# Attention beside a gated feed-forward layer: a shorter lead of row maxima, a lead job opened by the second lane, and new token orders

## The chip, the cores and the metric

The kernel runs on one core of a Trainium2 chip. A core has TensorE (PE in the profile; its weight loads are PEld), VectorE (DVE), ScalarE (ACT), GpSimd (POOL) and SyncE (SP), which here only issues DMAs. The metric is the device time of one execution in microseconds; lower is better.

## The reference

```python
# x: (1, 2048, 512), 32 heads of 16 that share one K and one V
q = (x @ wq) in heads;  k = x @ wk;  v = x @ wv
p = softmax(q k^T * 16 ** -0.5)          # per head, 2048 x 2048
a = (p v, heads side by side) @ wo
b = ((x @ w_gate) * (x @ w_up)) @ w_down # 1792 wide, no other nonlinearity
g = sigmoid((x * gate_w).sum(-1))
out = g * a + (1 - g) * b
```

## The kernel before

**Units.** The 2048 query rows are four chunks `c` of 512, each of four tiles `t` of 128. The 32 heads are four groups `g` of 8. A unit is (c, g, t), 64 in all. A unit's scores are computed twice. The first pass (`p1`, L800) multiplies queries by keys and lets DVE take the maximum of each row (L801, tile `mx`). The second pass (`p2`, L859) computes the transposed scores with the maximum subtracted: the negated maximum, in a high and a low part, stands as two more rows of `Q` beside the query, and the exponential is taken by ACT (L860, tile `P`). The product with V is `pv` (L872, tile `acc`).

**From the maxima to the second pass.** When 32 maxima of a unit are there (16 steps on each of two lanes), `p1_end` combines them on DVE (L809 to L815), four small DMAs store them to `dm` (L821), and two more fetch them into the extra rows of `Q` (L828). All of them go through SP's queue, which issues in order and waits at the first DMA that isn't ready. In the same queue stand the loads of weights (`wn`, `wdn`, L190), of queries (`Q<-dq`, L240), the stores of queries (`dq`, L224), the stores of the transposed x (`xd`, L373) and its reloads at a change of chunk (`xh`, `xl`, L213), and the steps of the softmax's division (`do`, `dn`, `raw`, `dr`, `rb`, L667 to L698).

**Lanes.** First and second pass need few contraction rows, so TensorE is used as two lanes: lane 0 takes rows 0 to 63, lane 1 rows 64 to 127, and the two run side by side. All other products (queries, gate, up, down, wo) are jobs of 12 steps a lane (L998, tile `ms`): each lane multiplies its half of the contraction rows, both add into one PSUM bank. Lane 0 opens a job's bank (`start`), lane 1 follows one job later and closes it (`stop`), then `evac` copies the bank out. So `count[1]` starts 12 steps after `count[0]`. The product with V takes all rows, so no lane runs beside it.

**The order of the work** is written out. One cycle of the token string `ORDER` covers one unit: `a`/`b` is a step of the first pass on lane 0/1, `c`/`d` one of the second pass, `e`/`f` a step of a job, `p` one round of `pv`. `APART` is a second string for cycles that take the jobs whose lanes write banks of their own. Runs of the first pass are ahead of the second: before the first cycle a lead loop puts `LEAD` steps of the first pass on each lane, six of them done earlier in the start-up, and beside them six jobs (`LEADJOBS`). In that loop a lane takes a step of the first pass whenever the planned DVE is less than 1.3 us behind, else a step of a job. In cycle u the second pass works on unit u and the first pass on what follows: with a lead of 25, the 16 steps of unit u + 1 are complete with the seventh `a` and `b` of the cycle. When the first pass runs out near the end, its tokens become job steps; after `npv` reaches `LASTORDER`, `end_token` chooses instead of the string.

**The planner.** While the program is written, a class `State` keeps planned times of lanes, DVE, ACT, POOL and banks, and a list of events puts DMAs and POOL work into the program order: `later(ns, fn)` and `at(t, fn)` issue `fn` once planned time has come. They set places in the queues, not waits on the chip. A second-pass token waits in planned time for `mat[u]`, the planned landing of the maxima, and a job is taken only if its weights are planned to be split (`ready`).

**Gate and up weights.** `order` lists (chunk, block of 128 columns). Job n has part 0 (gate) and part 1 (up). `ffn_stage` loads both weights, `ffn_split` splits each into a high and a low part on POOL (L152 and L153), and `evac` copies a part's result, multiplies the two on POOL (L599) and splits the product.

The tiles of `P` have 11 buffers (`PBUF`), those of `Q` five (`QB`).

Of the kernel before, what the change touches and what calls it, by code (L numbers as in the profile page):

```python
# [29 lines left out]
NJ = 16  # L30
# [1 line left out]
FG = 4  # L32
LAST = (0, 0, 1, 0, 1, 0)
YADDS = len(FGS) + 1 + sum(len(fs) < FG for fs in FGS)
LEAD = 25
PBUF = 11
WB = 4
QB = 5
# [17 lines left out]
SWAP = (10, 11, 12, 15)  # L56
LAT, LAT_LAST = 1.0, 0.5
LATE = 16
LEADJOBS = 6
O0, O1 = 0, 0  # L60


ORDER = (
    "cdebefedafebcfefcfcbefebedebcfefadefefcfafedebedebefedefadefcfafcfafefaf"
    "cfcdefebafedcpppbcbcbappdafafcfcfafafcfefedebedebefedebedefefafebadapppb"
)

APART = (
    "cedadfeeffaadfeedbedeedaffedeebedfcfacffafeefafcbfefccfafebcffceffabcfef"
    "ebefeedebbebapppbcdcdcppcbedfaeffcfadefefaebedeffcfadeebcfbeefbafedapppb"  # L70
)
SLOT = 1
COLS = (slice(0, 256), slice(256, 512))
# [6 lines left out]
def mix_kernel(ctx: ExitStack, tc: tile.TileContext, x, wq, wk, wv, wo, wg, wu, wd, gw, out):  # L80
    nc = tc.nc
# [111 lines left out]
    def w_split(n, tags, bufs, after=0.0):  # L193
        hi, lo = w512(tags[0], F32R, bufs), w512(tags[1], F32R, bufs)
        at = split2(hi, lo, n, after)
        return (hi, lo), at
# [20 lines left out]
    def at(t, fn):  # L217
        later(max(0.0, t - clock["T"]), fn)
# [9 lines left out]
    qat = {}  # L228
# [337 lines left out]
    def ffn_stage(i):  # L566
        if i < len(order):
            fs = slice(order[i][1] * 128, order[i][1] * 128 + 128)
            staged[i] = [stage(wg_v[:, :, fs]), stage(wu_v[:, :, fs])], clock["T"] + 4000.0

    def ffn_split(i):
        if i < len(order):
            ns, landed = staged.pop(i)
            W[i] = [w_split(n, ("wh", "wl"), WB, landed) for n in ns]
            at(W[i][1][1] + 300.0, lambda: ffn_stage(i + 2))

    def wd_split(wdn):
        if len(wdn) < 2:
# [2 lines left out]
    def ffn_job(n, i, gu, hat, wdn):  # L581
        c, f = order[n]

        def evac(p, part):
            gu[i] = w512("gs", F32, 3)
            if st["idle"]:
                nc.vector.tensor_copy(gu[i], p)
                end = spend("dve", RED)
            else:
                nc.scalar.copy(gu[i], p)  # L590
                end = spend("act", COPY)
            if len(gu) == 2:
                hf = w512("hf", F32, 1)
                h[f] = w512("hh", F32R, FG + 2), w512("hl", F32R, FG + 2)
                if st["idle"]:
                    nc.vector.tensor_tensor(hf, gu[0], gu[1], op=OP.mult)
                    spend("dve", 620.0, end + 200.0)
                else:
                    nc.gpsimd.tensor_tensor(hf, gu[0], gu[1], op=OP.mult)  # L599
                    spend("pool", 1240.0, end + 200.0)  # L600
                done = split2(h[f][0], h[f][1], hf)
                wd_split(wdn)
                wds[f], split_at = wdn[1]
                hat[f] = max(done, split_at) + 300.0
                if f == NF - 1 and c + 1 < NC:
                    x_turn(c + 1)
                ffn_split(n + 2)
                if n == len(order) - 4:
                    picks()
                    later(25000.0, wo_last)  # L610
        return Job(lambda: proj(W[n][i][0], xT[c]), evac,
                   lambda: max(W[n][i][1] + 300.0 if n in W else 1e18, xat.get(c, 1e18)))

    def down_jobs(c, fs, hat):
        n = FG // len(fs)
# [190 lines left out]
    def p1_end(u):  # L806
        q = Q[u]
        m = mm[u % 2]
        nc.vector.tensor_reduce(m[:, 0:8], mx.pop(u), axis=AX.X, op=OP.max)  # L809
        w = work.tile([128, 3, 32], F32R, name="mt", bufs=2)  # L810
        mt = w[:, 0].bitcast(F32)
        nc.vector.transpose(mt, m)
        nc.vector.tensor_reduce(w[:, 1], mt.rearrange("p (q v) -> p q v", v=1), axis=AX.X, op=OP.max, negate=True)
        with nc.allow_low_precision(reason="the low part of two that are kept"):
            nc.vector.tensor_reduce(w[:, 2], w[:, 0:2].bitcast(F32).rearrange("p v q -> p q v"), axis=AX.X, op=OP.add)  # L815
        end = spend("dve", 700.0)
        d = dram.tile([2, 8, 128], F32, name="dm", tag="dm", bufs=2)

        def store():
            for b in range(4):  # L820
                nc.sync.dma_start(d[:, :, b * 32:b * 32 + 32].rearrange("v c q -> c v q"),  # L821
                                  w[b * 32:b * 32 + 8, 1:3].bitcast(F32))
            later(3200, fetch)

        def fetch():
            for half in range(2):
                r = half * 64 + 48
                nc.sync.dma_start(q[r:r + 2].bitcast(F32), d[:, half * 4:half * 4 + 4, :])  # L828
            mat[u] = clock["T"] + 4000.0
        later(end - clock["T"] + 300.0, store)  # L830

    P = {}
# [124 lines left out]

    own, apart = {}, False

    def fill(l):  # L960

        c = count[l] + (O0, O1)[l]
        count[l] += 1
        k, i = c // 12 - l, c % 12
        wait = 0.0
        if i == 0 and l == 0:
            st["apart"] = apart and k % 3 == SLOT
            for _ in range(40):
                if peek():
                    break  # L970
                wait_ns(100.0)
            if peek():
                j = jobs[k] = take()
                j.items = j.prods()
                j.len = len(j.items) // j.parts
                if st["idle"]:
                    j.split()
                j.end, j.bank, j.p = [[None, None] for _ in range(j.parts)], {}, {}
            st["apart"] = False
        j = jobs.get(k)  # L980
        if j is None or i >= len(j.items):
            return
        part, i = divmod(i, j.len)
        if i == 0 and (l == 0 or j.apart):
            b = E.claim()
            wait, E.free[b] = E.free[b], 1e18
            j.bank[part] = b
            j.p[part] = ms_bank(b)
            if j.apart:
                own[l] = b, j.p[part]  # L990
        elif i == 0 and j.end[part][0] > E.known:
            fence()
        b, p = own[l] if j.apart else (j.bank[part], j.p[part])
        at = E.issue(l, wait)
        E.wrote[b] = E.seq
        lhs, rhs = j.items[part * j.len + i]
        end = i + 1 == j.len
        nc.tensor.matmul(p, lhs[HALVES[l]], rhs[HALVES[l]], start=(i == 0 and (l == 0 or j.apart)),  # L998
                         stop=(end and (l == 1 or j.apart)))
        if end:  # L1000
            j.end[part][l] = E.seq
            if part + 1 == j.parts and None not in j.end[part]:
                del jobs[k]
            if l == 1 or j.apart:
                clock["T"] = max(clock["T"], at)
                clock["act"], clock["dve"] = max(E.act, at + SEEN), max(E.dve, at + SEEN)
                if st["idle"]:
                    E.free[b] = clock["dve"] + RED_END + GAP
                    clock["act"] = E.act
                else:  # L1010
                    E.free[b] = clock["act"] + COPY_END + GAP
                    clock["dve"] = E.dve
                j.evac(p, part)
                E.act, E.dve = max(E.act, clock["act"]), max(E.dve, clock["dve"])
# [44 lines left out]
    def fillable(l):  # L1059
        c = count[l] + (O0, O1)[l]  # L1060
        if E.npv == 0 and count[l] >= 0 and min(E.n1) < LEAD:
            return False
        while st["idle"] and c % 12 and (c // 12 - l not in jobs or c % 12 >= len(jobs[c // 12 - l].items)):
            count[l] += 1
            c += 1
        if c % 12 == 0 and l == 0:
            return len(jobs) < (2 if min(E.n1) >= LEAD else 3) and peek() is not None
        j = jobs.get(c // 12 - l)
        if j is None or l == 0 or c % 12 % j.len > 0:
            return j is not None  # L1070
        end = j.end[c % 12 // j.len][0] if c % 12 < len(j.items) and not j.apart else 0
        return end is not None and end <= E.known

    count = [-12 * LEADJOBS - O0, -12 * (LEADJOBS - 1) - O1]
    while min(E.n1) < LEAD or min(count) < 0:
        l = 0 if E.nl[0] <= E.nl[1] else 1
        k = E.n1[l]
        some = k < LEAD and k <= E.n1[1 - l] + 2 and qat.get(order1[k][0], 1e18) <= clock["T"]
        if some and (E.dve < E.nl[l] + 1300.0 or not fillable(l)) and min(E.free) < E.nl[l]:
            token("ab"[l])  # L1080
        elif fillable(l):
            token("ef"[l])
        else:
            E.nl[l] += 30.0
            events_until(min(E.nl))
# [111 lines left out]
```

## Time and profile before

| what | us |
|---|---|
| median of 3 runs (lowest, highest) | 1596.78 (1596.07, 1596.89) |
| the profiled execution: its time, its span | 1597.58, 1595.6 |
| PE busy | 1590.0 |
| DVE busy, of this the row maxima (L801) | 1339.5, 1260.7 |
| ACT busy, of this the exponentials (L860) | 1203.5, 1067.8 |
| POOL busy | 719.5 |

The page names each group of instructions by line, engine, operation and tiles, with its count, busy time, the mean in ns, and what ended the engine's idle time before it. The granted TensorE clock is 0.999 of full speed. In the order of time a row has the start and the length in microseconds, and how many instructions are merged in it. A row of a stretch has the stretch, its length, the busy time of PE, PEld, DVE, ACT and POOL, each with its number of instructions, then the granted clock, the share of DMA time and GB/s. Matmuls overlap and their ends are modelled, so PE busy says little on how full its lanes are.

### The profile page before, as it was taken

How to read it: one execution, taken by the hardware profiler on the slowest of the kernel's cores; microseconds unless marked ns; L12 is line 12 of the kernel's file. 1: busy time of each engine (PE TensorE's matmuls, PEld its weight loads, DVE VectorE, ACT ScalarE, POOL GpSimd, SP SyncE). 2: the span in 40 equal slices, each digit the busy share in tenths (PEclk: the TensorE clock that was granted, in tenths of full speed). 3: DMA queues.
4: the chain of work that ended last, by engine and by line, in shares of the span. 5: the costliest groups of instructions: out<-in, count | busy, mean ns of one | idle time of the engine just before them, and what ended most of it. 6: DMA issues, size and time to landing. Idle time of an engine off the chain costs nothing.

```text
span 1595.6 us, 35607 instructions
## 1 busy us (share of the span) xinstructions
PE 1590.0 (100%) x13155; PEld 1046.0 (66%) x13155; DVE 1339.5 (84%) x2423; ACT 1203.5 (75%) x2360; POOL 719.5 (45%) x858
## 2 busy tenths in 40 slices
PE   9999999999999999999999999999999999999998
PEld 7766667666666666666666666666666666666664
DVE  6988888888888888888888888888888888888873
ACT  4577777777788777777788777777788777777775
POOL 3334653535643552534543650643743561553530
PEclk9999999999999999999999999999999999999999
DMA  4563322212311221212232221212231221221201
GB/s 157 188 205 112 107 62 65 57 54 78 116 54 51 76 75 45 76 49 61 80 101 62 77 69 50 77 49 63 77 102 48 74 73 55 66 67 42 56 29 46
DMA packets 185557, 121.68 MB, mean 76 GB/s; under 512 B 46378, under 2 KB 154998, under 8 KB 185384
## 3 DMA queue, kind: packets, MB, share of 16 engines
q1 hardware_dynamic: 184176, 119.21, 25.0%
q8 instruction: 104, 1.70, 0.5%
q14 instruction: 69, 0.57, 0.1%
q10 hardware_dynamic: 1208, 0.20, 0.1%
HBM read 82.96 MB, written 36.17 MB: 75 GB/s over the span
## 4 chain that ended last, share of the span: by engine, by line
PE 100%; DVE 0%; DVEq 0%; issue 0%
PE ms L998 36%; PE acc L872 29%; PE s L800 17%; PE s L859 16%; PE ms L165 1%; PE px L300 0%; PE px L285 0%; PE wo L1173 0%; PE warm L885 0%; PE pv L343 0%; PE warm L888 0%; DVE y L782 0%; DVEq L1193 0%; PE sums L752 0%; PE pv L355 0%
## 5 line engine op out<-in xcount | busy, mean ns | idle before, releaser
L801 DVE TENSOR_REDUCE mx<-s 128x1 f32<-128x512 f32 x2048 | 1260.7, 683 | 205.0 <-PE s L859 141.8
L860 ACT ACTIVATE P<-s 128x512 f32<-128x512 f32 x2048 | 1067.8, 630 | 196.2 <-PE s L800 95.8
L859 PE MATMUL s<-Q,KK 50*128 50x512 f32 x2044 | 713.7, 405 | 0.0
L800 PE MATMUL s<-KK,Q 48*128 48x512 f32 x2048 | 711.8, 406 | 0.2 <-issue 0.2
L872 PE MATMUL acc<-P,V 128*32 128x512 f32 x4096 | 480.1, 597 | 0.0
L800 PEld LDWEIGHTS s<-KK,Q 48*128 48x128 f32 x2048 | 347.4, 185 | 141.2 <-issue 46.8
L859 PEld LDWEIGHTS s<-Q,KK 50*128 50x128 f32 x2044 | 354.8, 185 | 85.7 <-issue 53.8
L998 PE MATMUL ms<-xh,wh 64*128 64x512 f32 x920 | 322.2, 394 | 0.0
L998 PE MATMUL ms<-xh,wl 64*128 64x512 f32 x920 | 321.9, 391 | 0.0
L998 PE MATMUL ms<-xl,wh 64*128 64x512 f32 x920 | 307.8, 391 | 0.0
L872 PEld LDWEIGHTS acc<-P,V 128*32 128x32 f32 x4096 | 113.4, 109 | 253.1 <-issue 232.7
L599 POOL TENSOR_TENSOR hf<-gs 128x512 f32<-128x512 f32 x56 | 72.0, 1285 | 372.3 <-ACT gs L590 361.2
L412 POOL TENSOR_TENSOR y<-y,yt 128x512 f32<-128x512 f32 x67 | 85.6, 1283 | 217.0 <-ACT yt L410 213.8
L998 PEld LDWEIGHTS ms<-xh,wh 64*128 64x128 f32 x920 | 161.4, 186 | 14.0 <-POOL wl L153 0.2
L998 PEld LDWEIGHTS ms<-xh,wl 64*128 64x128 f32 x920 | 159.4, 186 | 10.0
L998 PE MATMUL ms<-wdh,hh 64*128 64x512 f32 x448 | 159.7, 396 | 0.0
L998 PEld LDWEIGHTS ms<-xl,wh 64*128 64x128 f32 x920 | 154.0, 185 | 8.8
L998 PE MATMUL ms<-wdh,hl 64*128 64x512 f32 x448 | 158.0, 392 | 0.0
L998 PE MATMUL ms<-wdl,hh 64*128 64x512 f32 x448 | 155.3, 392 | 0.0
L153 POOL TENSOR_TENSOR wl<-wn,wh 128x512 fp32r<-128x512 f32 x117 | 150.7, 1288 | 9.4
L876 ACT COPY osb<-acc 128x512 f32<-128x512 f32 x64 | 37.6, 588 | 139.5 <-PE acc L872 139.5
L998 PEld LDWEIGHTS ms<-wdh,hh 64*128 64x128 f32 x448 | 79.7, 185 | 6.7 <-ACT P L860 0.4
(171 smaller groups left out, 1267.7 us busy)
## 6 DMA issues: line engine op xcount, KB each, us to landing
do<-osb SPq DMA_DIRECT2D x63, 256.0 KB
wn<-in_B_w_gate_dram SPq DMA_DIRECT2D x56, 256.0 KB
wn<-in_B_w_up_dram SPq DMA_DIRECT2D x56, 256.0 KB
wdn<-in_B_w_down_dram SPq DMA_DIRECT2D x56, 256.0 KB
Q<-dq SPq DMA_DIRECT2D x384, 32.0 KB
raw<-do SPq DMA_DIRECT2D x252, 32.0 KB
dq<-oh SPq DMA_DIRECT2D x16, 256.0 KB
dq<-ol SPq DMA_DIRECT2D x16, 256.0 KB
```

Source lines behind the costliest of these rows:

```text
L153: nc.gpsimd.tensor_tensor(lo, src, hi.bitcast(F32), op=OP.subtract)
L165: nc.tensor.matmul(p, l, r, start=start and i == 0, stop=stop and i == len(prods) - 1)
L412: nc.gpsimd.tensor_tensor(y[c, t], y[c, t], tmp, op=OP.add)
L599: nc.gpsimd.tensor_tensor(hf, gu[0], gu[1], op=OP.mult)
L800: nc.tensor.matmul(p, q[r, slot], KK[r, kq * 512:(kq + 1) * 512], start=True, stop=True)
L801: nc.vector.tensor_reduce(mx[u][:, half * 4 + slot, kq:kq + 1], p, axis=AX.X, op=OP.max)
L859: nc.tensor.matmul(p, kj, q[r].rearrange("p s q -> p (s q)"), start=True, stop=True)
L860: nc.scalar.activation(P[s][:, half], p, AF.Exp, scale=0.25)
L872: nc.tensor.matmul(acc[u][b:b + 32, :], V[:, j + i], src[:, half], start=(j == 0), stop=(j == NJ - 2))
L876: nc.scalar.copy(osb, acc.pop(u))
L998: nc.tensor.matmul(p, lhs[HALVES[l]], rhs[HALVES[l]], start=(i == 0 and (l == 0 or j.apart)), stop=(end and (l == 1 or j.apart)))
```

## The change

- `LEAD` is 21. The first 16 of these steps are taken as before; the other five are spread over the last 36 job steps of lane 0 (`PACED`), unless no job step can be issued.
- The lead jobs have an order per lane (`LEADS`). Lane 0 takes -6, -4, -3, -2, -5, -1, lane 1 takes -5, -6, -4, -3, -2 and, after the lead, -1. Job -5 is opened by lane 1 and closed by lane 0, which `first` tells in `fill` and `fillable`; all others are opened by lane 0 as before.
- Both strings are new. With a lead of 21, the steps of unit u + 1 are complete with the eleventh `a` and `b` of cycle u.
- The gate weights of job n + 2 are split on POOL at the first `evac` of job n, and the up weights at the second, ahead of the down weights.
- The planned time from storing the maxima to fetching them is 2600 and not 3200, and from there to their landing 3000 and not 4000.

```diff
-LEAD = 25
+LEAD = 21
+PACED = 36
-LEADJOBS = 6
+LEADS = (-6, -4, -3, -2, -5, -1), (-5, -6, -4, -3, -2, -1)
+LEADJOBS = len(LEADS[0])
 ORDER = (
-    "cdebefedafebcfefcfcbefebedebcfefadefefcfafedebedebefedefadefcfafcfafefaf"
-    "cfcdefebafedcpppbcbcbappdafafcfcfafafcfefedebedebefedebedefefafebadapppb"
+    "adadefebcfefadefcfebededafefcfebebcfefedafefedebedafefcbefededebcfebefcf"
+    "ebcfafafafcfafcfppcbfebcdefeebedefcbefcfebedefadefafafcfefadpppcdababppp"
 APART = (
-    "cedadfeeffaadfeedbedeedaffedeebedfcfacffafeefafcbfefccfafebcffceffabcfef"
-    "ebefeedebbebapppbcdcdcppcbedfaeffcfadefefaebedeffcfadeebcfbeefbafedapppb"
+    "dafcbedefeafedebdebeedebdefefcbefccfafaffcfafefdeafeffcebcfefbcfeafaffcf"
+    "eadefefcfafedfafeabfebapppcbadcbcppcbdebedeebedefefadefebcfedfedafecbppp"
...
-    def ffn_split(i):
+    def ffn_split(i, parts=range(2)):
         if i < len(order):
-            ns, landed = staged.pop(i)
-            W[i] = [w_split(n, ("wh", "wl"), WB, landed) for n in ns]
-            at(W[i][1][1] + 300.0, lambda: ffn_stage(i + 2))
+            ns, landed = staged[i]
+            for part in parts:
+                W.setdefault(i, []).append(w_split(ns[part], ("wh", "wl"), WB, landed))
+            if len(W[i]) == 2:
+                at(W[i][1][1] + 300.0, lambda: ffn_stage(i + 2))
...
+            if len(gu) == 1:
+                ffn_split(n + 2, (0,))
             if len(gu) == 2:
...
                 done = split2(h[f][0], h[f][1], hf)
+                ffn_split(n + 2, (1,))
                 wd_split(wdn)
...
-                ffn_split(n + 2)
...
-            later(3200, fetch)
+            later(2600, fetch)
...
-            mat[u] = clock["T"] + 4000.0
+            mat[u] = clock["T"] + 3000.0
...
+    def place(l):
+        c = count[l] + (O0, O1)[l]
+        k = c // 12 - l
+        if k < 0:
+            k = LEADS[l][k]
+        return k, c % 12, int(k == LEADS[1][0])
...
-        if i == 0 and (l == 0 or j.apart):
+        if i == 0 and (l == first or j.apart):
...
-            return len(jobs) < (2 if min(E.n1) >= LEAD else 3) and peek() is not None
+        k, i, first = place(l)
+        if i == 0 and l == first:
+            return (k < 0 or len(jobs) < 2) and peek() is not None
...
-        some = k < LEAD and k <= E.n1[1 - l] + 2 and qat.get(order1[k][0], 1e18) <= clock["T"]
+        due = NJ + (LEAD - NJ) * (1 + count[0] / PACED)
+        some = k < LEAD and (k < max(NJ, due) or not any(map(fillable, range(2)))) and k <= E.n1[1 - l] + 2 and qat.get(order1[k][0], 1e18) <= clock["T"]
```

More of the change, by code (lines that the diff above doesn't have):

```diff
@@ L611, in ffn_job @@
         return Job(lambda: proj(W[n][i][0], xT[c]), evac,
-                   lambda: max(W[n][i][1] + 300.0 if n in W else 1e18, xat.get(c, 1e18)))
+                   lambda: max(W[n][i][1] + 300.0 if len(W.get(n, ())) > i else 1e18, xat.get(c, 1e18)))
     def down_jobs(c, fs, hat):
@@ L958, in mix_kernel @@
     own, apart = {}, False
+    def place(l):
[4 more added lines that the diff above has]
+        return k, c % 12, int(k == LEADS[1][0])
     def fill(l):
-        c = count[l] + (O0, O1)[l]
+        k, i, first = place(l)
         count[l] += 1
-        k, i = c // 12 - l, c % 12
         wait = 0.0
-        if i == 0 and l == 0:
+        if i == 0 and l == first:
             st["apart"] = apart and k % 3 == SLOT
@@ L990, in fill @@
                 own[l] = b, j.p[part]
-        elif i == 0 and j.end[part][0] > E.known:
+        elif i == 0 and j.end[part][first] > E.known:
             fence()
@@ L997, in fill @@
         end = i + 1 == j.len
-        nc.tensor.matmul(p, lhs[HALVES[l]], rhs[HALVES[l]], start=(i == 0 and (l == 0 or j.apart)),
-                         stop=(end and (l == 1 or j.apart)))
+        nc.tensor.matmul(p, lhs[HALVES[l]], rhs[HALVES[l]], start=(i == 0 and (l == first or j.apart)),
+                         stop=(end and (l != first or j.apart)))
         if end:
@@ L1003, in fill @@
                 del jobs[k]
-            if l == 1 or j.apart:
+            if l != first or j.apart:
                 clock["T"] = max(clock["T"], at)
@@ L1065, in fillable @@
             c += 1
-        if c % 12 == 0 and l == 0:
-            return len(jobs) < (2 if min(E.n1) >= LEAD else 3) and peek() is not None
-        j = jobs.get(c // 12 - l)
-        if j is None or l == 0 or c % 12 % j.len > 0:
+        k, i, first = place(l)
+        if i == 0 and l == first:
+            return (k < 0 or len(jobs) < 2) and peek() is not None
+        j = jobs.get(k)
+        if j is None or l == first or i % j.len > 0:
             return j is not None
-        end = j.end[c % 12 // j.len][0] if c % 12 < len(j.items) and not j.apart else 0
+        end = j.end[i // j.len][first] if c % 12 < len(j.items) and not j.apart else 0
         return end is not None and end <= E.known
```

## The prediction

> **What bounds the kernel now.** I read the page first (shares of busy time, the chain that ended last, the costliest groups), then stretches of the span side by side, then the order of time around the lead, a cycle's end and a late maximum.
>
> ```profile
> PE 1590.0 (100%) x13155; PEld 1046.0 (66%) x13155; DVE 1339.5 (84%) x2423; ACT 1203.5 (75%) x2360; POOL 719.5 (45%) x858
> PE 100%; DVE 0%; DVEq 0%; issue 0%
> L801 DVE TENSOR_REDUCE mx<-s 128x1 f32<-128x512 f32 x2048 | 1260.7, 683 | 205.0 <-PE s L859 141.8
> L998 PEld LDWEIGHTS ms<-xh,wh 64*128 64x128 f32 x920 | 161.4, 186 | 14.0 <-POOL wl L153 0.2
> ```
>
> The chain that ended last lies on TensorE alone, so time is won only where its two lanes (row halves 0-63 and 64-127) are filled better. What a filled pair of lane steps costs, and what a whole cycle costs, is read here: first two neighbouring rows of the order of time with both lanes full, then stretches.
>
> ```profile
> 1580.73 0.45 PE L998 MATMUL ms<-wdh,hl 64*128 64x512 f32 x2
> 1580.96 0.45 PE L998 MATMUL ms<-wdl,hh 64*128 64x512 f32 x2
> ...
> 54.80:79.85 25.05, 25.05 (x203) 15.80 (x202) 21.84 (x38) 18.40 (x36) 7.69 (x9) 1.00 0.68 244
> ...
> 558.78:582.58 23.80, 23.80 (x206) 15.57 (x202) 20.48 (x37) 18.38 (x36) 19.22 (x22) 1.00 0.30 86
> 247.06:270.95 23.89, 23.89 (x204) 15.84 (x200) 20.52 (x37) 18.30 (x36) 9.26 (x11) 1.00 0.21 61
> 438.07:462.62 24.55, 24.55 (x204) 15.65 (x201) 20.63 (x37) 20.21 (x39) 10.88 (x12) 1.00 0.21 60
> ```
>
> A pair of steps takes 1580.96 - 1580.73 = 0.23 us. An ordinary cycle (one token string, one unit) takes 23.89, a good one 23.80, one with the APART string 24.55, and the first cycle 25.05. In all of them PE reads as 100% busy: the loss hides inside "busy", and only the length tells it.
>
> The lead, the stretch before the first cycle, is next: PE in two equal windows, PE's first and last steps of it, its transposes for V, then DVE.
>
> ```profile
> 32.10:38.10 6.00, 6.00 (x41) 4.99 (x41) 5.76 (x10) 1.16 (x4) 2.34 (x2) 1.00 0.00 0
> 38.10:44.10 6.00, 6.00 (x58) 5.79 (x56) 6.00 (x11) 0.94 (x4) 1.44 (x2) 1.00 0.02 5
> ...
> 32.09 0.49 PE L998 MATMUL ms<-xh,wh 64*128 64x512 f32 x1
> ...
> 37.69 0.27 PE L355 MATMUL pv<-ident,gs 64*128 64x64 f32 x1
> ...
> 38.18 0.47 PE L800 MATMUL s<-KK,Q 48*128 48x512 f32 x1
> ...
> 54.78 0.49 PE L859 MATMUL s<-Q,KK 50*128 50x512 f32 x1
> ...
> 32.66 12.16 DVE L801 TENSOR_REDUCE mx<-s 128x1 f32<-128x512 f32 x20 [0.23 <-PE s L800]
> ...
> 45.67 19.88 DVE L801 TENSOR_REDUCE mx<-s 128x1 f32<-128x512 f32 x32
> ```
>
> In the first 6 us PE issues 41 matmuls, in the next 6 us 58: lane 1 has no job yet, since it follows lane 0 by one job. DVE reduces without a break, 12.16 / 20 = 0.61 us a maximum. The lead runs from 32.09 to the first second-pass matmul at 54.78, 22.7 us.
>
> **The change, part by part.** The sum is made against the profiled execution, 1597.58 us (span 1595.6), which is 0.8 above the median of the three runs, 1596.78.
>
> *Lead of 21 and lane 1's own job.* Six steps of each lane are done before the lead, so it holds 21 - 6 = 15 maxima per lane and not 19, plus 72 job steps on lane 0 and 60 on lane 1. Lane 0 then needs 15 + 72 = 87 steps x 0.23 = 20.0, and 0.5 for the transposes (37.69 to 38.18): 20.5 us. DVE needs 30 x 0.61 = 18.3, so it isn't the limit any more (before: 38 x 0.61 = 23.2, about the 22.7 seen). The lead is 2.2 us shorter. The 4 maxima per lane left out of it are done later, where they push 4 pairs of job steps to the end: 4 x 0.23 = +0.9. Net **-1.3**. Ends: 0, if lane 1, with 12 fewer steps, idles as much at the end as it did at the start and lane 0 waits for DVE; -2.2, if the four steps fall into idle slots of the last cycles.
>
> *The first cycle* took 25.05 where a later one takes 23.89, so 1.2 too much, with DVE still working off the lead (the row of 32 reductions runs unbroken from 45.67 to 65.55). With DVE no longer the limit of the lead I take half, **-0.6**; ends 0 and -1.2.
>
> *New strings.* Both old and new ORDER have 144 tokens: 16 each of a, b, c, d, 36 of e, 36 of f, and 8 of p in three bursts. Nothing is added or removed, so the sum of work is the same and only stalls can change. They are bounded by the ordinary cycle against the good one: 23.89 - 23.80 = 0.09 a cycle, x 55 ordinary cycles (64, less the first, two at the end and six with APART) = -5.0. Upward the nearest row is an APART cycle: 24.55 - 23.89 = 0.66, x 55 = +36. What queues where can be counted off the strings. Before the first burst, the last 14 tokens (7 pairs, 1.6 us) held five exponentials and two maxima; now three and four. ScalarE's pile there is smaller, DVE's is larger, but the burst of matmuls that follows lets both drain. In the next stretch the first ten tokens held three maxima, after four in the six tokens of `bcbcba`; now two, right after a burst. The pile that a lane meets in mid-stretch is a bit lower, so I lean to the good cycle's row and take half of its gain, 0.045 x 55 = **-2.5**. The new APART has its six cycles' 0.66 to win or to double: 6 x 0.66 = 4.0 both ways, taken as 0.
>
> *The later maxima.* This is where the edit can hurt. Rows: an ordinary unit, a unit with the reload of x ahead of it in the queue, and an early unit. Each begins with the unit's last maximum (L800) and ends with the first second-pass matmul of that unit (L859).
>
> ```profile
> 231.42 0.39 PE L800 MATMUL s<-KK,Q 48*128 48x512 f32 x1
> ...
> 232.86 0.19 DVE L809 TENSOR_REDUCE mm<-mx 128x8 f32<-128x32 f32 x1
> ...
> 233.79 1.29 SPq L821 DMA_DIRECT2D dm<-mt  x4
> 236.12 0.53 SPq L828 DMA_DIRECT2D Q<-dm  x2
> ...
> 247.06 0.50 PE L859 MATMUL s<-Q,KK 50*128 50x512 f32 x1
> ...
> 1165.41 0.39 PE L800 MATMUL s<-KK,Q 48*128 48x512 f32 x1
> ...
> 1166.73 1.75 SPq L213 DMA_DIRECT2D xh<-xd  x4
> 1168.58 1.80 SPq L213 DMA_DIRECT2D xl<-xd  x4
> 1170.42 4.15 SPq L240 DMA_DIRECT2D Q<-dq  x6
> 1175.42 3.17 SPq L821 DMA_DIRECT2D dm<-mt  x4
> 1179.64 0.53 SPq L828 DMA_DIRECT2D Q<-dm  x2
> ...
> 1180.97 0.50 PE L800 MATMUL s<-KK,Q 48*128 48x512 f32 x1
> 1181.03 0.50 PE L859 MATMUL s<-Q,KK 50*128 50x512 f32 x1
> ...
> 88.14 0.39 PE L800 MATMUL s<-KK,Q 48*128 48x512 f32 x1
> ...
> 97.95 1.18 SPq L828 DMA_DIRECT2D Q<-dm  x2
> ...
> 92.81:93.71 0.90, 0.90 (x11) 0.49 (x7) 0.36 (x1) 0.33 (x1) 0.68 (x3) 1.00 0.30 81
> 101.02 2.71 PE acc L872 x24
> ```
>
> Before, the last maximum of a unit was the 7th `a` of its cycle and 247.06 - 231.42 = 15.6 us were left. Now it is the 11th, token 118, with 14 tokens, a burst of three, six tokens and a burst of three behind it: 7 x 0.23 + 0.1 + 2.71 + 0.90 + 2.71 = 8.0 us, because the second token of the new string is already a `d`. Needed are 236.12 - 231.42 = 4.7 up to the fetch, and 1181.03 - 1179.64 = 1.4 from the fetch to a second-pass matmul that had just waited for it (0.06 behind lane 0, with which it otherwise starts): 6.1, and 0.2 for a longer DVE queue. Cover left: 1.7 us, where it was 9.5. On that matmul hang both lanes and the P tiles of the unit. In an ordinary cycle nothing is paid. The early unit took 97.95 - 88.14 = 9.8 to the fetch, 5.1 more than usual, with x stores and q stores ahead of it on SP: over the cover by 3.4. The new store falls some 7 us later, when these thin out; **+0.5**, ends 0 and 6.8 (two such units).
> The Trainium skill, "DMA: Bandwidth & Descriptors", section "Anatomy of one DMA — SWDGE (gpsimd) path", gives a DMA a fixed cost of about 2.0 us, most of it the receipt of the write; it states this for the other path. By that figure the cover would be an estimated 1.1 and this term about +1.5. The row's 1.4 covers both transfers (0.53 to issue the two), so the trace speaks for less.
>
> *Planner constants 2600 and 3000.* They move no work: they place the fetch earlier on SP's list, and let the second pass of the plan begin sooner. Cost 0, the cover being the 1.7 us above; without it the price is the rival's below.
>
> *Gate weights one job ahead.* The rows of the two POOL instructions:
>
> ```profile
> L153 POOL TENSOR_TENSOR wl<-wn,wh 128x512 fp32r<-128x512 f32 x117 | 150.7, 1288 | 9.4
> L152 POOL CAST wh<-wn 128x512 fp32r<-128x512 f32 x117 | 71.5, 611 | 2.8 <-DMA wn<-in_A_wq_dram 1.9 <-PE s L800 0.9
> ```
>
> The same 0.61 + 1.29 us are queued after the first copy of a job instead of after its product; up weights now precede down weights, so the latter are ready 1.9 us later and the wn loads are asked for earlier on SP. PE waited 0.2 us in all for wl, and POOL is busy 45%: 0. If that cover went, one job of 12 lane steps would slip, 12 x 0.23 = 2.8 us.
>
> *Sum:* -1.3 - 0.6 - 2.5 + 0.5 = -3.9. Profiled execution 1593.7, median 1592.9.
>
> **The rivals.**
> *A, slower: the maxima come late.* SP is one list in order; a transfer ahead of `dm` or `Q<-dm` that waits for ACT, POOL or a buffer holds them up. The unit at a chunk's turn took 1179.64 - 1165.41 = 14.2, 9.5 over the usual; over the new cover by 7.8. Three turns are 23.4 and two early units 6.8: +30, or 1623 in full. For it: eight such 256 KB transfers plus Q<-dq do hold the queue from 1166.73 to 1174.6. Against: that ends 6.4 us before the cycle's end at 1180.97, and the new store is due 5.4 before it. It decides from 1.7 us of delay per unit, and makes the kernel slower by 0.2% once the lateness sums to 7.1 us. In the Trainium skill, "TensorE: Matmul & The Clock Gate", section "Part 3: Packing small matmuls — row/col tiling", matmuls start strictly in program order; by that a late half stops both lanes and the lateness is paid in full. The trace fits: after 1181.03 no lane has run ahead.
> *B, no change: the strings stall as before.* Then only -1.3 - 0.6 + 0.5 = -1.4 is left: 1595.4. For it: 23.89 against 23.80 is little to win, and the counts of the two strings are close. Against: a cycle of 23.80 has the same work.
> *C, the new string stalls more*, 0.1 a cycle: +5.5 - 1.4, 1600.9. For it: four maxima, 2.4 us of reduction, in the last 1.6 us before a burst. It decides when DVE's pile reaches the bank that PE needs.
>
> **How the numbers follow.** About 0.2%, 3.2 us, is what a measurement of this kernel can tell. My forecast has 0.55: 0.43 faster by over 0.2%, 0.12 within it; its own range is 1589.5 to 1594.8. B has 0.22, within. A has 0.16 and C 0.07, slower. So 0.43, 0.34, 0.23. The range goes from 1588 (all of the lead, first cycle and 5.0 of the strings would be 1589.3, with a little of APART) up to 1601, which takes in C and A up to 8 us.
>
> **What would show it.** The first L859 near 52.6 instead of 54.78; the first 6 us from 32.1 with nearer 55 PE records; the first cycle about 24.4; ordinary cycles of 23.85 or less between second bursts; `Q<-dm` about 3 us before the cycle's end, and L859 starting with L800 there. Wrong would be L859 behind L800 by more than 0.1 at cycle starts, mainly around 100 and 1181 us and at the other chunk turns (A), or cycles of 23.9 (B) and 24.0 (C).

## The result, and the profile after

The changed kernel is slower: 1620.6 us in the median against 1596.6, ratio 1.0151 [1.0123, 1.0178]. Predicted was 1592.9, with 0.23 for slower. The median is that of three executions; the one profiled at first took 8850 us, with every TensorE instruction four to five times as long as in all others, and is left out, so the profile "after" is that of the same kernel run again (experiment `e1_again`, profiled at 1622.32 us, span 1620.5).

In the changed kernel the lines named in the prediction have moved: first pass L800 is L806, maxima L801 is L807, second pass L859 is L865, the store `dm` L821 is L827, the fetch `Q<-dm` L828 is L834, weights L190 is L192, queries `Q<-dq` L240 is L242, reload of x L213 is L215, and the job steps L998 are L1010. The end of the chain on DVE, L809 to L815, is L815 to L821.

From the page: busy times, the chain that ended last by engine and by line, and the group of the second pass, whose last column is the idle time before it and what ended it.

```profile
PE 1600.7 (99%) x13155; PEld 1057.6 (65%) x13155; DVE 1353.9 (84%) x2421; ACT 1201.6 (74%) x2361; POOL 721.9 (45%) x859
...
PE 92%; DMA 3%; SPq 3%; POOL 1%; issue 1%; DVE 0%; ACT 0%; DVEq 0%; POOLq 0%
...
L865 PE MATMUL s<-Q,KK 50*128 50x512 f32 x2044 | 760.0, 410 | 14.7 <-DMA Q<-dm 12.4
```

Before, the chain was PE 100%. Now 8% of it lies on DMA, SP's queue, POOL and issue, and the second pass alone waited 12.4 us for `Q<-dm`, which no line of before shows. The page says what was waited for; the stretches say in which cycles. First the two windows of the lead, then the first cycle, an ordinary one, a late one and its successor, the one before a chunk's turn, and one with the APART string (columns as before: the tenth group is the granted clock).

```profile
32.10:38.10 6.00, 6.00 (x44) 4.54 (x42) 4.87 (x9) 0.92 (x4) 2.10 (x2) 1.00 0.00 0
38.10:44.10 6.00, 5.96 (x57) 5.82 (x57) 6.00 (x12) 0.94 (x4) 1.21 (x2) 1.00 0.01 3
...
52.70:78.05 25.35, 25.35 (x205) 15.47 (x201) 21.34 (x37) 18.76 (x36) 8.76 (x9) 1.00 0.59 210
...
154.18:178.06 23.88, 23.88 (x205) 15.52 (x201) 20.70 (x37) 18.20 (x36) 13.14 (x16) 1.00 0.27 77
273.78:301.28 27.50, 25.85 (x205) 17.23 (x201) 21.26 (x37) 18.64 (x36) 16.92 (x20) 0.94 0.22 64
301.28:325.26 23.98, 23.98 (x205) 15.63 (x201) 20.59 (x37) 18.27 (x36) 11.08 (x14) 1.00 0.20 55
422.77:448.76 25.99, 23.93 (x204) 15.48 (x201) 20.69 (x37) 18.86 (x37) 12.54 (x15) 1.00 0.46 145
...
1226.88:1251.23 24.35, 24.35 (x204) 15.70 (x201) 20.56 (x37) 19.94 (x39) 9.48 (x11) 1.00 0.17 50
```

The account between the two profiled executions follows from three points of time in each. The first cycle ends at 78.05 where it ended at 79.85 (-1.8). Cycles 1 to 61 take 1487.35 us instead of 1460.72 (+26.6). What comes after is equal, 55.1. The sum is +24.9, the difference of the spans. And the 26.6 are not spread out: an undisturbed cycle is 23.9, as before, but 16 of the 61 are at least 0.3 longer than the same cycle of a run without lateness (`e7_lead23` below), together by 24.8 (the other 1.8 are small: 1.2 that this run has over before too, and 0.6).

Why a cycle is late shows when a late unit and the one after it are laid side by side in the order of time: POOL, DVE's last instruction on the maxima, SP's queue, then PE at the start of the cycle.

```profile
265.19 1.30 POOL L155 TENSOR_TENSOR wl<-wn,wh 128x512 fp32r<-128x512 f32 x1
...
267.55 0.22 DVE L821 TENSOR_REDUCE mt<-mt 128x32 fp32r<-128x64 f32 x1
...
266.51 0.38 SPq L192 DMA_DIRECT2D wn<-in_B_w_up_dram  x1
266.99 3.65 SPq L242 DMA_DIRECT2D Q<-dq  x6
270.74 1.29 SPq L827 DMA_DIRECT2D dm<-mt  x4
274.14 0.53 SPq L834 DMA_DIRECT2D Q<-dm  x2
...
273.78 0.49 PE L806 MATMUL s<-KK,Q 48*128 48x512 f32 x1
275.93 0.47 PE L865 MATMUL s<-Q,KK 50*128 50x512 f32 x1 [1.65 <-DMA Q<-dm]
...
295.03 0.22 DVE L821 TENSOR_REDUCE mt<-mt 128x32 fp32r<-128x64 f32 x1
...
289.38 2.87 SPq L242 DMA_DIRECT2D Q<-dq  x6
295.29 1.29 SPq L827 DMA_DIRECT2D dm<-mt  x4
297.62 0.53 SPq L834 DMA_DIRECT2D Q<-dm  x2
...
301.28 0.49 PE L806 MATMUL s<-KK,Q 48*128 48x512 f32 x1
301.28 0.50 PE L865 MATMUL s<-Q,KK 50*128 50x512 f32 x1
```

In both units DVE is done with the maxima 6.0 us before the cycle's end (267.77 and 295.25, against 273.78 and 301.28). In the unit that is on time the store is issued at once and the fetch 2.33 us later. In the late one SP stood at the load of up weights until POOL had finished a `wl` at 266.49, which freed the buffer. Then came the six fetches of queries, which the program issues after the same step of the first pass that completes the maxima. They hold the queue until 270.64, so `dm` waits 2.97 us in it, and from store to fetch it is 3.40 us instead of 2.33. From the fetch to the matmul it is 1.79 us: 2.97 + 3.40 + 1.79 = 8.16 of the 6.01 us there are, and the second pass starts 2.15 us late (275.93 - 273.78). With 0.04 and 2.33 for the first two terms the unit on time would need 4.16, so the cover is 1.85 us: the 1.7 of the prediction was right.

The weight load is not the only thing that stops SP there. In 15 of the 16 late units the six fetches of queries stand next ahead of `dm` (in the other, the first, a store of the transposed x lies between). Ahead of the fetches stands in eight units the load of up weights, which waits for POOL, in six the step `dr` of the softmax's division, which waits for DVE (L700, tile `rc`), and in the two early ones stores of the transposed x. The waits of SP's own queue, with the totals, the times and the longest in us, show how often it stood at the load and at the division (first the changed kernel, then the kernel before):

```profile
SPq L192 <- POOL wl L155: 232.4, 59, 8.7
SPq L700 <- DVE rc L695: 165.7, 36, 11.6
...
SPq L694 <- DVE rc L689: 165.7, 56, 8.8
SPq L190 <- POOL wl L153: 68.8, 29, 4.7
```

The totals are idle time of a queue, which costs nothing by itself. The longest waits matter: a stop of 8 to 10 us ahead of the six fetches pushes them into the moment when the maxima are ready.

### The profile page after: what moved, and what is told of

It reads as the page before. It is cut to its first block, busy times and chain, and to the rows that moved or that the text cites. A ratio compares the mean times of both kernels' runs of the same rounds, so it can differ in the third digit from the quotient of the medians.

```text
span 8848.6 us, 35530 instructions
## 1 busy us (share of the span) xinstructions
PE 8844.4 (100%) x13155; PEld 4366.0 (49%) x13155; DVE 1489.4 (17%) x2421; ACT 1403.5 (16%) x2361; POOL 714.5 (8%) x859
## 4 chain that ended last, share of the span: by engine, by line
PE 100%; issue 0%; DVE 0%
PE ms L1010 34%; PE acc L878 31%; PE s L806 17%; PE s L865 16%; PE ms L167 1%; PE px L302 0%; PE wo L1187 0%; PE px L287 0%; PE pv L345 0%; PE warm L891 0%; PE warm L894 0%; PE sums L758 0%; PE pv L357 0%; PE pick L758 0%; DVE y L788 0%
## 5 line engine op out<-in xcount | busy, mean ns | idle before, releaser
L865 PE MATMUL s<-Q,KK 50*128 50x512 f32 x2044 | 3296.0, 1718 | 0.0
L806 PE MATMUL s<-KK,Q 48*128 48x512 f32 x2048 | 3134.4, 1698 | 0.0
L878 PE MATMUL acc<-P,V 128*32 128x512 f32 x4096 | 2721.2, 2950 | 0.0
L807 DVE TENSOR_REDUCE mx<-s 128x1 f32<-128x512 f32 x2048 | 1404.0, 691 | 7089.3 <-PE s L806 4020.9
L865 PEld LDWEIGHTS s<-Q,KK 50*128 50x128 f32 x2044 | 1739.4, 886 | 1073.1 <-issue 999.8
L806 PEld LDWEIGHTS s<-KK,Q 48*128 48x128 f32 x2048 | 1673.5, 887 | 715.4 <-issue 551.0
L1010 PE MATMUL ms<-xh,wh 64*128 64x512 f32 x920 | 1375.5, 1708 | 0.0
L1010 PE MATMUL ms<-xh,wl 64*128 64x512 f32 x920 | 1343.7, 1668 | 0.0
L1010 PE MATMUL ms<-xl,wh 64*128 64x512 f32 x920 | 1325.2, 1685 | 0.0
L1010 PEld LDWEIGHTS ms<-xh,wl 64*128 64x128 f32 x920 | 782.2, 952 | 140.6 <-issue 140.6
L1010 PEld LDWEIGHTS ms<-xh,wh 64*128 64x128 f32 x920 | 726.7, 882 | 194.5 <-issue 194.1
L1010 PEld LDWEIGHTS ms<-xl,wh 64*128 64x128 f32 x920 | 713.8, 894 | 171.4 <-issue 171.4
L1010 PE MATMUL ms<-wdh,hh 64*128 64x512 f32 x448 | 679.3, 1702 | 0.0
L1010 PE MATMUL ms<-wdh,hl 64*128 64x512 f32 x448 | 662.6, 1669 | 0.0
L1010 PE MATMUL ms<-wdl,hh 64*128 64x512 f32 x448 | 659.2, 1684 | 0.0
L1010 PEld LDWEIGHTS ms<-wdh,hl 64*128 64x128 f32 x448 | 380.9, 941 | 78.8 <-issue 78.8
L1010 PEld LDWEIGHTS ms<-wdh,hh 64*128 64x128 f32 x448 | 360.9, 884 | 99.2 <-issue 98.3
L1010 PEld LDWEIGHTS ms<-wdl,hh 64*128 64x128 f32 x448 | 359.4, 899 | 86.4 <-issue 86.4
```

The lines of the kernel that those rows point to most:

```text
L806: nc.tensor.matmul(p, q[r, slot], KK[r, kq * 512:(kq + 1) * 512], start=True, stop=True)
L807: nc.vector.tensor_reduce(mx[u][:, half * 4 + slot, kq:kq + 1], p, axis=AX.X, op=OP.max)
L865: nc.tensor.matmul(p, kj, q[r].rearrange("p s q -> p (s q)"), start=True, stop=True)
L878: nc.tensor.matmul(acc[u][b:b + 32, :], V[:, j + i], src[:, half], start=(j == 0), stop=(j == NJ - 2))
```

## The experiments

In the texts on record, A is the theory that the maxima come late through SP's queue; the others are named where they occur.

**The same kernel again.**

> The changed kernel once more, for a profile at TensorE's usual pace. Theory A (the later maxima miss the second pass): about 1620 us again; the first second-pass matmul of a unit (L865) starts after lane 0's first step at many cycle starts, and these waits sum to some 20 to 30 us; cycles without such a wait last 23.9 us or less. Theory C (the new strings stall more): 1620 us too, but the loss is spread as 0.4 us over every cycle, inside its long stretches, and L865 starts on time. Theory D (that chip ran TensorE badly and the time was not the kernel's): about 1593 us.

1619.84 us, ratio 1.0149 [1.0133, 1.0164]. The slowdown is the kernel's, as theories A and C had it and D had not; that it sits in late cycles and not in all of them speaks for A against C. The views above are of this run.

**The lead alone put back.**

```diff
-LEAD = 21
+LEAD = 25
```

> The changed kernel with LEAD 25 and all else as changed (PACED, LEADS, both strings, gate split, 2600 and 3000). The last maximum of a unit is then the seventh a or b of the new string, about 14.7 us before the next cycle and not 8.0. Theory A: the loss goes away, 1590 to 1597 us. Theory C: the strings are the same, so it stays near 1620 us.

1600.71, ratio 1.0027 [1.0016, 1.0038]. Of the 23 us 19 are gone, and no cycle's second pass starts late. What is left, 4 us over before, was not expected (A's range was 1590 to 1597). In the profiled execution the first cycle holds 1.9 of it and the six APART cycles, which take 24.8 to 24.9, another 1.9. That execution was the slowest of the seven (1602.65; the others 1600.4 to 1600.73), so the first cycle's share may be its own. Three stretches of its trace:

```profile
54.64:81.62 26.98, 26.77 (x202) 17.00 (x200) 23.57 (x41) 18.57 (x35) 7.59 (x8) 0.94 0.66 238
...
54.00:56.00 2.00, 1.90 (x9) 1.01 (x9) 2.00 (x4) 0.62 (x2) 0.08 (x1) 1.00 0.22 56
...
58.00:60.00 2.00, 2.00 (x14) 1.56 (x12) 2.00 (x5) 1.45 (x3) 0.89 (x2) 0.50 1.03 382
```

With 25 steps DVE is the lead's limit again: from 54 to 56 it is busy throughout and PE gets 9 matmuls in 2 us instead of some 17. Soon after, the granted clock is 0.50, and the first cycle takes 26.98. So this run ends the lateness, but is no clean measure of the new strings. Its first second-pass matmul stands at 54.64, where before has 54.78: lane 1's own lead job, with the lead as long as before, gains 0.14.

**Both old strings, lead 21.** The two strings are those of before, the rest is the changed kernel.

```diff
 ORDER = (
-    "adadefebcfefadefcfebededafefcfebebcfefedafefedebedafefcbefededebcfebefcf"
...
+    "cdebefedafebcfefcfcbefebedebcfefadefefcfafedebedebefedefadefcfafcfafefaf"
...
```

> The changed kernel with both strings of before, LEAD 21 and the rest as changed. The eleventh a of the old string is its token 116, so the maxima are as late as with the new ones (about 8 us before the cycle's end), and c and d are its first two tokens. Theory A: slow as well, 1610 to 1640 us. Theory C: the old strings bring the old cycles back, 1593 to 1598 us.

1651.04, ratio 1.0341 [1.0326, 1.0357]. The number is above A's range, and A's reason is not the one. (In the expectation I counted the eleventh `a` of the old string as token 116. It is token 99, counted from 0, which leaves 8.1 us, as much as the new string.) Nearly all cycles start on time: five of cycles 1 to 61 are more than 0.3 us late, and all lateness sums to 4.1 us of the 54.0 that these cycles lose. Instead every ordinary cycle is some 0.8 us longer, 24.69 where before has 23.89, and all of that lies in one stretch, between the second and the third product with V. That stretch, on DVE and PE, and the cycle:

```profile
269.36 0.19 DVE L815 TENSOR_REDUCE mm<-mx 128x8 f32<-128x32 f32 x1
...
270.05 0.22 DVE L821 TENSOR_REDUCE mt<-mt 128x32 fp32r<-128x64 f32 x1
270.19 2.48 DVE L807 TENSOR_REDUCE mx<-s 128x1 f32<-128x512 f32 x4
...
270.93 0.49 PE L806 MATMUL s<-KK,Q 48*128 48x512 f32 x1 [0.23 <-DVE mx L807]
...
251.77:276.46 24.69, 24.46 (x205) 15.38 (x202) 20.48 (x37) 18.44 (x36) 12.21 (x14) 1.00 0.20 59
```

With 21 steps of lead the unit's maxima are complete right behind the place where the old string puts four first-pass steps into six tokens (`bcbcba`) and a product with V after them. DVE has a pile of maxima there, and now closes the unit too: 269.36 to 270.27, 0.9 us in which it reduces none. A first-pass matmul then stands on PE until a maximum has freed its bank. That reading is argued from the place of the loss; it makes the new strings and the lead of 21 belong together, through DVE.

**The gate split and the planner's two times alone, on the kernel before.**

```diff
+            if len(gu) == 1:
+                ffn_split(n + 2, (0,))
...
+                ffn_split(n + 2, (1,))
                 wd_split(wdn)
...
-                ffn_split(n + 2)
...
-            later(3200, fetch)
+            later(2600, fetch)
...
-            mat[u] = clock["T"] + 4000.0
+            mat[u] = clock["T"] + 3000.0
```

> The kernel before with the gate weights split one job ahead and the planner's 2600 and 3000, and nothing else of the change. Theories A and C: nothing on the path moves, 1596.6 us within 2. A theory E, that the reordered POOL and SP queues are the cause by themselves: about 1615 to 1620 us.

1596.37, ratio 0.9999 [0.999, 1.0009]. Nothing, as predicted.

**The gate split put back, the rest changed.**

```diff
-            if len(gu) == 1:
-                ffn_split(n + 2, (0,))
...
-                ffn_split(n + 2, (1,))
                 wd_split(wdn)
...
+                ffn_split(n + 2)
```

> The changed kernel with gate and up weights both split at the second evac again, as before the change; lead, strings and planner constants as changed. Theory A1 (the load of the up weights, which waits on SP for POOL's split of the up weights, is what holds up the maxima, and the early gate split put it there): most of the 24 us goes, 1597 to 1604 us. Theory A2 (the cover of under 2 us is too thin for whatever stands ahead in SP's list, the query fetch first of all): it stays slow, 1610 to 1625 us.

1620.84, ratio 1.015 [1.0136, 1.0164]: the total is the same without the split, so the split is not needed for the loss. But other units pay. SP waited half as long for POOL at the weight loads (121.5 us against 232.4) and longer for DVE at the division's step (250.3 against 165.7). One cycle at a chunk's turn, 33.15 long, holds 8.6 us of the loss: its second pass starts 7.27 late, since its `dm` stood 8.7 us behind the reload of x and the fetches of queries. That is what A had priced, at 7.8 a turn. The second-pass matmul that waits there (L863 in this kernel), and the cycle:

```profile
449.50 0.76 PE L863 MATMUL s<-Q,KK 50*128 50x512 f32 x1 [6.77 <-DMA Q<-dm]
...
442.23:475.38 33.15, 26.35 (x204) 17.13 (x201) 21.08 (x37) 18.95 (x36) 10.37 (x13) 0.90 0.21 63
```

**The fetches of queries taken from in front of the maxima.** All else is the changed kernel; the planned delay of those six DMAs grows so that they come behind `dm` and `Q<-dm` in SP's order.

```diff
-            later(1500, lambda n=fetched: q_fetch(n))
+            later(9000, lambda n=fetched: q_fetch(n))
```

> The changed kernel with one number changed: a unit's query fetch (Q<-dq, six DMAs, 2.8 us of issue on SP) is put on the list 9000 and not 1500 planned ns after the step that triggers it, so that it stands behind the maxima's store and fetch and not ahead of them. Both theories A1 and A2 say the late maxima cost the 24 us; if the query fetch between the blocked load and the store is what makes them late, dm<-mt is issued 0.7 us after the DVE transpose in nearly all cycles and the time falls to 1593 to 1599 us. If it is the blocked load itself, under a quarter of the loss goes: above 1612 us.

1599.05, ratio 1.0014 [1.0005, 1.0023]. One number takes away 21 of the 23 us, to just above the range expected. SP's wait for POOL at the weight loads is a fifth less than in the changed kernel, with a longest one just as long, but hardly matters now. Three units are late: unit 2, near 100 us, by 2.3, and units 3 and 19 by 0.5 and 0.8. In front of unit 2's `dm` stand stores of the transposed x. The row of SP's wait, that unit's stores, its store of the maxima and its second pass:

```profile
SPq L192 <- POOL wl L155: 185.3, 52, 8.6
...
95.52 3.53 SPq L375 DMA_DIRECT2D xd<-wol  x3
99.14 1.31 SPq L827 DMA_DIRECT2D dm<-mt  x4
...
104.20 0.47 PE L865 MATMUL s<-Q,KK 50*128 50x512 f32 x1 [1.84 <-DMA Q<-dm]
```

**A lead of 23.** The maxima are complete two first-pass steps of each lane sooner, with the ninth `a` and `b` instead of the eleventh, and some 14 us of the cycle are left instead of 8.

```diff
-LEAD = 21
+LEAD = 23
```

> The changed kernel with LEAD 23. The unit's last maximum is then the ninth a or b of the new string, 14 us and not 8 before the next cycle. If the cover is what counts: no second-pass matmul starts late, 1596 to 1600 us (between the measured 1600.7 of LEAD 25 and the 1595 that the lead of 21 would give without lateness). If the new strings need a lead of 21 for DVE's sake, some 0.3 us in every cycle are lost where the transposes of the maxima fall into the pile before the burst: above 1612 us.

1597.28, ratio 1.0002 [0.9993, 1.0011]. Nothing is late. SP's wait at the weight loads falls as well (to 82.7 us, longest 4.2), so this run alone doesn't part cover from a freer queue; with the run before, in which only the order changed, it does. It is also the clean measure of the new strings. Two ordinary cycles of it:

```profile
126.21:150.13 23.92, 23.92 (x205) 15.00 (x201) 20.60 (x37) 18.18 (x36) 13.86 (x17) 1.00 0.36 109
269.67:293.55 23.88, 23.88 (x205) 15.23 (x202) 20.63 (x37) 18.18 (x36) 16.89 (x20) 1.00 0.25 73
```

They are what the old strings gave (23.89). Cycles 1 to 61 take 1461.93, 1.2 more than before.

**The shorter lead on the old strings.** Old strings, old place of the split, old planner times; `LEADS` and `PACED` as changed, and a lead of 24.

```diff
-LEAD = 21
+LEAD = 24
...
-            later(2600, fetch)
+            later(3200, fetch)
```

> The kernel before (its strings, its gate split, its planner times) with lane 1's own lead job, the spread of the last steps, and LEAD 24. The last maximum is the eighth a of the old string, 14.6 us before the next cycle, so nothing is late. If the lead is where the change gains, the first second-pass matmul starts about 1 us earlier than 54.78 and the time is 1594.5 to 1596 us. If a lead job on lane 1 gains nothing, 1596.5.

1596.85, ratio 1.0 [0.9991, 1.0009]. The first cycle ends 0.9 us sooner than before (78.92), by the end of cycle 61 the lead is 1.2, and when the last cycle ends it is 0.5: what the lead saves is spent at the end, and the rest is below what can be told.

**Query fetches late, and the stores of x spread.** The late query fetches again, with the stores of the transposed x set wider apart, since they stood in front of the one late unit:

```diff
-        later(35000.0 + 1200.0 * i, f)
+        later(35000.0 + 3000.0 * i, f)
```

> e6 with the 24 early stores of the transposed x spread over 72 instead of 29 planned us (3000 and not 1200 ns apart), so that they no longer stand in a block ahead of unit 2's maxima. In e6 unit 2's second pass began 2.3 us late and its cycle took 27.66 and not 23.9; the half of the extra that is more than the lateness went with a granted clock of 0.88. Theory (lateness is all that is left, and the idle gap costs clock on top): 1594.5 to 1596.5 us, below both kernels by 0.5 to 2 us. Rival (the stores move the lateness to units 1 and 3): 1598 to 1602 us.

1599.40, ratio 1.0015 [1.0005, 1.0024]: missed. Of the three late units two are left, units 2 and 3, late by 0.7 and 0.8, so the lateness did shrink, but the time did not. It lies in the range of the rival, whose reason the trace bears out only in part: unit 3 is later than it was, unit 1 is on time. The profiled execution took 1598.55, the others up to 1600.3. Where the rest of the 2.5 us over before goes stays open.

**Query fetches late, on the kernel before.**

```diff
-            later(1500, lambda n=fetched: q_fetch(n))
+            later(9000, lambda n=fetched: q_fetch(n))
```

> The kernel before with the later query fetch alone (9000 and not 1500). Its maxima have some 9 us of cover, so the queue's order should not matter: 1596.5 to 1597 us, no change. If the later fetch is a gain of its own, apart from the lateness: below 1594 us.

1597.54, ratio 1.0004 [0.9994, 1.0013]. With 9.5 us of cover the order in SP's queue is worth nothing. So the same edit is worth 21 us with the thin cover and none with the wide one.

**Old strings, lead 23,** an edit of the run with the old strings. The maxima are complete earlier, so lateness should go; DVE's pile should stay.

```diff
-LEAD = 21
+LEAD = 23
```

> e3 (both strings of before, the rest as changed) with LEAD 23 and not 21. The last maximum of a unit is then the ninth a of the old string, its token 93, with 10.5 us to the next cycle and not 8.1, so lateness is ruled out. In e3 every cycle lost 0.8 us in its second long stretch, and cycle starts were on time. Theory P (the transposes that close a unit's maxima, 0.9 us on DVE, fall into the pile of maxima after the first burst, and PE waits for a bank): still there at token 93, since the pile bcbcba is tokens 88 to 93; over 1610 us. Theory A (lateness in some hidden form): gone, 1596 to 1600 us.

1625.93, ratio 1.0181 [1.0164, 1.0198]. Ordinary cycles are on time at their start, 24.29 long, and again it is the second long stretch that takes more. Unlike what was expected, lateness is not ruled out: two of cycles 1 to 61 start 0.9 and 1.7 us late, and the second of these takes 28.07. But all lateness sums to 3.0 us of the 30.3 that these cycles lose. The waits of PE's weight loads for maxima, with totals, times and the longest, in this run and before:

```profile
PEld s L806 <- DVE mx L807: 49.2, 62, 0.8
PEld s L865 <- DVE mx L807: 40.5, 141, 0.8
...
PEld s L800 <- DVE mx L801: 23.4, 29, 0.8
```

The wait of the second pass for a maximum doesn't occur in the kernel before. So lateness is not the main cause with the old strings, and the rows fit a pile on DVE. With a lead of 24 (the run on the old strings above) the maxima are complete at token 80, ahead of the pile that begins at token 88, and nothing is lost. That it is the closing of the unit on DVE, and nothing else that moves with the lead, is not shown apart.

## Why the prediction was wrong, point by point

- **The lead: right.** 2.2 us shorter was forecast; the first second-pass matmul stands at 52.70 instead of 54.78, 2.1 sooner. The four later steps were to cost 0.9 at the end; the stretch after cycle 61 takes 55.1 in both, so that charge is not seen there. The forecast of 55 matmuls in the first 6 us was wrong (44; the second window has 57). The lead got shorter because DVE had fewer maxima to do, not because PE started full: with the same lead jobs the first second-pass matmul stands at 54.64 with a lead of 25, at 53.40 with 23 and at 52.70 with 21.
- **The first cycle: wrong.** -0.6 forecast, 25.35 against 25.05 measured. So the gain at its end is 1.8 in all, against 2.8 forecast.
- **New strings: wrong by the whole term.** -2.5 was half of what separates an ordinary cycle from a good one. The lead of 23 shows the new strings undisturbed, the two cycles above at 23.92 and 23.88: +1.2 over 61 cycles. B's term was right. Counting exponentials and maxima off the strings didn't say what a lane meets. What it did not ask is where the unit's closing on DVE (0.9 us) falls; the old strings with leads of 23 and 21 lose 0.4 and 0.8 us a cycle, which fits it.
- **The later maxima: the step that failed.** +0.5 was forecast, with ends of 0 and 6.8, and A was held down to 0.16. Measured are 24.8 us in 16 cycles. The cover was right (1.7, measured 1.85), though not each part of it: from the fetch to a matmul that waits for it the late units show 1.79 and, at the chunk's turn below, 1.80 us, not 1.4. (The 2.0 of the Trainium skill, "DMA: Bandwidth & Descriptors", "Anatomy of one DMA — SWDGE (gpsimd) path", which is stated for another path, was the nearer figure.) Wrong was the sentence "In an ordinary cycle nothing is paid." It rested on one unit, at 231 us, in which SP's queue happened to be free when the maxima came, with 9.5 us of cover behind it; a wait that is covered leaves no trace to be noticed. Two things were in the kernel and not in the working: the fetch of queries is tied to the very step that completes the maxima, and six of its DMAs take 2.8 us or more, above the cover on their own; and what stands ahead of them waits for another engine, in the kernel before the weight load for POOL 29 times, up to 4.7 us, and the division's step for DVE 56 times, up to 8.8. Those rows were to be had, and both are above 1.7.
- **Rival A: right in mechanism and, partly by luck, in its sum.** "1623 in full" stands against 1620.6. It was made of three chunk turns at 7.8 and two early units at 3.4. In the profiled execution two of the turns cost 2.1 and 1.6 and the second one, at 836.64, nothing; the two early units cost 1.2 and 3.3. The other 16.7 are twelve ordinary cycles that A had not named. The argument against it, that the reload of x ends before the store is due, failed in its own place as well. SP and PE at the first turn:

```profile
432.99 1.77 SPq L215 DMA_DIRECT2D xh<-xd  x4
434.86 1.80 SPq L215 DMA_DIRECT2D xl<-xd  x4
...
439.83 2.84 SPq L242 DMA_DIRECT2D Q<-dq  x6
442.76 2.87 SPq L827 DMA_DIRECT2D dm<-mt  x4
446.96 0.53 SPq L834 DMA_DIRECT2D Q<-dm  x2
...
448.76 0.49 PE L865 MATMUL s<-Q,KK 50*128 50x512 f32 x1 [2.06 <-DMA Q<-dm]
```

  The reload is over at 436.66, early as argued; the query fetch behind it runs to 442.67, `dm` takes 2.87 to issue and 4.20 to the fetch, and the cycle starts 2.06 late.
- **Both lanes stop together: right.** After 448.76 no lane has run ahead, and in the late cycle above lane 0 starts one matmul at 273.78 and PE then stands for 1.65 us. The lateness is paid nearly in full (1.3 us for 1.43 late in the cycle at 617.43) or with more (3.6 for 2.15). The trace agrees with the Trainium skill, "TensorE: Matmul & The Clock Gate", "Part 3: Packing small matmuls — row/col tiling", by which matmuls start in program order.
- **Gate split and planner constants: right, 0.** 0.9999 [0.999, 1.0009] alone, and the same total loss without the split.
- **APART: nearly right, 0 forecast.** The six cycles are 0.03 to 0.24 us shorter than the same six before, 0.6 in all (the last of them 24.35 here, 24.49 before).

Without lateness, then, the change is worth nothing that can be told: 1597.28 with the lead of 23, 1599.05 with the queries out of the way. No version run was faster than the kernel before beyond the interval.

## What to carry to other kernels

When a result is made later, its cover must be held against the worst state of the in-order queue that it goes through, and not against one unit in which that queue was free: list what the program puts in front of it, what of this waits for another engine, and what is triggered by the same step. A wait that is still covered before the change is the one to look up, with its longest case. And an order tuned for one lead is tuned for where every periodic small task falls; here the new lead with the old order cost 54 us, more than the two together (24).

## What was not expected of the hardware

Some late cycles cost more than their lateness, because the clock falls after the wait. The stretch from the late start in the run with late query fetches, the part of it from 1.5 us after the restart, the same 44 pairs of tokens in an undisturbed cycle of the same run, and the part of that from 1.5 us after its start:

```profile
101.86:116.19 14.33, 12.49 (x93) 11.40 (x89) 10.97 (x20) 10.88 (x21) 2.36 (x3) 0.88 0.61 193
...
105.70:109.20 3.50, 3.50 (x20) 3.46 (x19) 2.36 (x4) 2.73 (x6) 0.00 (x0) 0.52 0.48 138
...
153.77:164.34 10.57, 10.57 (x92) 8.51 (x89) 10.04 (x17) 10.28 (x21) 3.84 (x5) 1.00 0.52 152
...
155.27:158.77 3.50, 3.50 (x32) 2.92 (x32) 3.50 (x7) 3.50 (x8) 0.51 (x2) 1.00 0.79 241
```

The second pass is 2.3 us late and PE idle for 1.84 of it, but the stretch is 3.76 longer. The rows of 3.5 us show where the rest goes: from 1.5 us after the restart the granted clock is 0.52 for 3.5 us, and that stretch holds 20 matmuls where the undisturbed one (last row) holds 32. The late cycle above (27.50 for 2.15 late, clock 0.94) pays in the same way; three of the 16 late cycles do (at 103.11, 273.78 and 933.19; the others show a clock of 1.00), and they hold 10.4 of the 24.8 us for some 6.1 us of lateness. Not every execution shows it: the changed kernel's executions have a mean granted clock of 0.997 to 1.000, and the one at 1.000 still took 1620.56 us, so the loss does not need the clock. With the lead of 25 PE was hardly idle (1.90 of 2.00 us busy), only fed 9 matmuls in 2 us, and the clock was 0.50 in 58.00:60.00. The Trainium skill, "TensorE: Matmul & The Clock Gate", "Part 1: The HAM clock gate (the "warmup" mystery)", tells of a free-running window of some 3.4 us after which an idle array gets half the clock; the length of the dip agrees, but its rule of no idle gaps above some 3.4 us is too mild for these rows. Nor is it the gap's length alone. After the 2.06 us idle ahead of 448.76 the next cycle, one with the APART string, ran at full clock:

```profile
448.76:473.25 24.49, 24.49 (x202) 15.75 (x202) 20.48 (x37) 19.78 (x38) 10.79 (x12) 1.00 0.14 43
```

With a free-running window it would depend on where the gap falls in it; no run here tested that.
